# A share of the attention masks moved from TensorE to GpSimd, and the squared norms from GpSimd to ScalarE

## Chip, cores and metric

The kernel runs on one core of a Trainium2 chip. The metric is the device time of one execution in microseconds (us). A core has five engines that run side by side, each through its own queue of instructions in order: TensorE (matrix products, PE in the profile, with its weight loads as PEld), VectorE (DVE), ScalarE (ACT), GpSimd (POOL) and SyncE (SP, which here issues DMA transfers). The engines wait for each other through semaphores.

## What is computed

A block-sparse attention is followed by a layer of experts in which each token goes to one of eight.

```python
# q, k, v: (B=4, H=8, S=768, D=64) float32; 24 blocks of 32 tokens
scores = scale * np.matmul(q, k.transpose(0, 1, 3, 2))
mask = np.abs(blk_i - blk_j) <= 1                      # neighbouring blocks
mask = mask | (blk_i == 0) | (blk_j == 0) | (blk_i == 23) | (blk_j == 23)
#      ... and three sampled key blocks for each query block
attn = softmax(np.where(mask, scores, -1e9)) @ v
x = attn.transpose(0, 2, 1, 3).reshape(3072, 512)
# routing: cosine of each row with 8 expert vectors, softmax, best expert
xn = x / (np.linalg.norm(x, axis=-1, keepdims=True) + 1e-06)
logits = xn @ en.T / tau
expert_idx = np.argmax(logits, axis=1);  gate_w = softmax(logits)[.., expert_idx]
for e in range(8):
    out[rows of e] = gate_w * (np.maximum(x[rows of e] @ w1[e], 0) @ w2[e])
```

The mask is the same for all batches and heads. The scores are small, so the kernel takes the exponential without subtracting a maximum.

## The kernel before

The work of the attention is cut into 192 **units**. One unit is one pair of heads, one half of the queries (384) and one chunk of the keys (128). Six units (kc = 0 to 5) make a **half**: all keys for one pair of heads and one half of the queries. There are 32 halves; eight halves (48 units) make a **sequence**, that is, one of the four batches. A unit has two TensorE parts, `score_fast` and `attend_fast`. Between them stands the exponential on ScalarE.

```python
def score_fast(k, u):
    ps = k.big.tile([P, 2, 512], F32, name="sc", tag="big")        # PSUM, 2 buffers
    quarters = [(h, r, ...) for r in range(2) for h in range(2)]
    for rows, cols, first in ((k.kmask, k.qmask, True), (kt, qt, False)):
        for h, r, keys in quarters:       # mask product in bf16, then scores in f32, summed in PSUM
            nc.tensor.matmul(ps[D*r:D*(r+1), h, 0:HALF], lhsT=rows[D*h:D*(h+1), keys],
                             rhs=cols[D*h:D*(h+1), queries], start=first, stop=not first)
    e = k.ep.tile([P, 2, HALF], F32, name="e", tag="e")            # SBUF, 4 buffers
    k.exps = nc.scalar.activation(e, ps[:, :, 0:HALF], ACT.Exp, scale=SCALE)

def attend_fast(k, u):
    # kc == 0: k.av = new PSUM tile (1 buffer); kc == 1: esum = first + e
    k.summed = nc.vector.tensor_tensor(out=k.esum, in0=k.esum, in1=e, op=ALU.add)
    for r in range(2):
        for h in range(2):
            nc.tensor.matmul(k.av[D*h:D*(h+1), r, 0:HALF], lhsT=v[..., h, kc, :], rhs=e[D*r:D*(r+1), h, :],
                             start=(kc == 0), stop=(kc == NC - 1))
    if kc == NC - 1:
        nc.scalar.copy(out=part, in_=k.av[:, 1, 0:HALF])
        k.summed = nc.vector.tensor_tensor(out=at, in0=k.av[:, 0, 0:HALF], in1=part, op=ALU.add)
```

The mask product adds a large negative number to the scores of forbidden blocks, so that their exponential is zero. `settle` then turns a finished half back to rows with tokens on partitions (36 small matmuls), and divides by the sums of the exponentials. `squares` adds up the squares of the new rows for the norm.

```python
def settle(k, w):
    ...                                                            # 12 + 24 matmuls into PSUM "back"
    nc.vector.reduce_sum(out=den.rearrange(...), in_=sums, axis=AX.X)
    nc.vector.tensor_scalar(out=den, in0=den, scalar1=1e-9, scalar2=None, op0=ALU.add)
    nc.vector.reciprocal(out=inv..., in_=den)
    nc.vector.tensor_tensor(out=k.x[b][...], in0=rows[:, :, :, 0:D], in1=inv..., op=ALU.mult)
    nc.vector.tensor_tensor(out=k.part[b][...], in0=rows[:, :, :, D:W], in1=inv..., op=ALU.mult)

def squares(k, w):                                                 # the last half uses ScalarE instead
    nc.gpsimd.tensor_tensor(out=sq, in0=x, in1=x, op=ALU.mult)     # 128 x 384
    width = P // 2
    while width:                                                   # 7 steps of a tree, 192 down to 3
        nc.gpsimd.tensor_tensor(out=out, in0=sq[:, :, 0:width], in1=sq[:, :, width:2*width], op=ALU.add)
        width //= 2
```

The main loop keeps the scores two units ahead. In the first unit of a half the score stands ahead of the other part, because the one buffer of `av` must first be read out by `at`.

```python
for u in range(units):
    if u % NC == 3 and ...: settle(n, u // NC - 1)
    if u % NC == 4 and ...: squares(n, u // NC - 1)
    for when, what in plan: ...                                    # routing and dispatch of the sequence before
    steps = [partial(attend_fast, n, u)] + ([partial(score_fast, n, u + 2)] if u + 2 < units else [])
    for step in reversed(steps) if u % NC == 0 else steps:
        step()
    if u % per - ... in (0, 1): turn_blocks(...)                   # DVE transposes of the next pair
```

After the attention come 25 **tiles** of 128 rows each: gather the rows of one expert, two products with its weights (`hp`, `yp`), scatter the result. Four more tiles stand behind a condition and run only if the routing needs them; `last_tiles` then fetches their rows itself.

```python
def fetch(k, i):
    if i + 2 < k.stop and i + 2 != NE:
        fetch_rows(k, i + 2)             # late tiles: four indirect DMAs on GpSimd
```

Of the kernel before, what the change touches and what calls it, by code (L numbers as in the profile page):

```python
# [45 lines left out]
XE = P + 1  # L46
XW = ND * XE
SCALE = 1.0 / float(D) ** 0.5
HALF = S // 2
NQ = HALF // P  # L50
DEN_LOW, DEN_HIGH = 0.1, 1e10
NEG = -1.0e9


class Net:
# [3 lines left out]
def two_banks(k, name):  # L59
    return k.small.tile([P, 2, 512], F32, name=name, tag="small")  # L60
# [300 lines left out]
def score_fast(k, u):  # L361

    nc = k.nc
    g, qh, kc = u // (2 * NC), u // NC % 2, u % NC
    kt, qt = k.turned[g]
    ps = k.big.tile([P, 2, 512], F32, name="sc", tag="big")
    queries = slice(qh * HALF, (qh + 1) * HALF)
    quarters = [(h, r, slice(kc * P + D * r, kc * P + D * (r + 1))) for r in range(2) for h in range(2)]
    for rows, cols, first in ((k.kmask, k.qmask, True), (kt, qt, False)):
        for h, r, keys in quarters:  # L370
            nc.tensor.matmul(ps[D * r:D * (r + 1), h, 0:HALF], lhsT=rows[D * h:D * (h + 1), keys],  # L371
                             rhs=cols[D * h:D * (h + 1), queries], start=first, stop=not first)
    e = k.ep.tile([P, 2, HALF], F32, name="e", tag="e")
    k.exps = nc.scalar.activation(e, ps[:, :, 0:HALF], ACT.Exp, scale=SCALE)  # L374
    k.es[u] = e


def attend_fast(k, u):
# [24 lines left out]
def settle(k, w):  # L403

    nc = k.nc
    at, esum = k.done.pop(w)
    g, qh = w // 2, w % 2
    b, j = g // NPAIR, g % NPAIR
    if w % (2 * NPAIR) == 0:
        k.x[b] = k.xp.tile([P, NC, ND, XE], F32, name="x", tag="x")  # L410
        k.nsq[b] = k.xp.tile([P, NC, NPAIR], F32, name="nsq", tag="nsq")
        k.part[b] = k.xp.tile([P, NC, H, E], F32, name="part", tag="part")
    ps = two_banks(k, "back")
    W = D + E
    rows = ps[:, :, 0:NQ * W].rearrange("p h (t w) -> p t h w", t=NQ)
    sums = ps[:, :, NQ * W:NQ * W + 2 * NQ].rearrange("p r (t h) -> p t h r", t=NQ)
    for t in range(NQ):
        for h in range(2):
            for s in range(2):
                cols = slice(t * P + D * s, t * P + D * (s + 1))  # L420
                nc.tensor.matmul(rows[D * s:D * (s + 1), t, h, :], lhsT=at[D * h:D * (h + 1), cols],  # L421
                                 rhs=k.back[D * h:D * (h + 1), j, :], start=True, stop=True)
    for t in range(NQ):
        for h in range(2):
            for r in range(2):
                for s in range(2):
                    cols = slice(t * P + D * s, t * P + D * (s + 1))
                    nc.tensor.matmul(sums[D * s:D * (s + 1), t, h, r:r + 1], lhsT=esum[D * r:D * (r + 1), h, cols],  # L428
                                     rhs=k.ones[D * r:D * (r + 1), 0:1], start=True, stop=True)
    den = k.dens[:, w, :]  # L430
# [10 lines left out]
    nc.vector.tensor_tensor(out=k.part[b][:, chunks, 2 * j:2 * j + 2, :], in0=rows[:, :, :, D:W],  # L441
                            in1=inv.unsqueeze(3).broadcast_to([P, NQ, 2, E]), op=ALU.mult)


def squares(k, w):

    nc = k.nc
    b, j, qh = w // (2 * NPAIR), w // 2 % NPAIR, w % 2
    chunks = slice(qh * NQ, (qh + 1) * NQ)
    x = k.x[b][:, chunks, j, 0:P]  # L450
    sq = k.sp.tile([P, NQ, P], F32, name="sq", tag="sq", bufs=1)
    nc.gpsimd.tensor_tensor(out=sq, in0=x, in1=x, op=ALU.mult)  # L452
    width = P // 2
    while width:
        out = sq[:, :, 0:width] if width > 1 else k.nsq[b][:, chunks, j:j + 1]
        k.squared = nc.gpsimd.tensor_tensor(out=out, in0=sq[:, :, 0:width], in1=sq[:, :, width:2 * width],  # L456
                                            op=ALU.add).ins
        width //= 2


def last_squares(k, w):

    b, j, qh = w // (2 * NPAIR), w // 2 % NPAIR, w % 2
    for c in range(qh * NQ, (qh + 1) * NQ):
        sq = k.sp.tile([P, P], F32, name="sq_l", tag="sq_l")
# [508 lines left out]
def after_sequence(n, b):  # L974

    routing = partial(next, route(n, b), None)
    plan = [(7, routing), (14, routing), (16, routing), (17, routing), (20, partial(rank, n, b)), (23, routing)]
# [12 lines left out]


def attention_fast(n, ctx):
    def pool(name, bufs, **kw):
        return ctx.enter_context(n.tc.tile_pool(name=name, bufs=bufs, **kw))

    n.acc, n.big = pool("acc", 1, space=PSUM), pool("big_f", 2, space=PSUM)
    n.ld, n.tp, n.ep = pool("ld", 3), pool("tp", 2), pool("ep", 4)
    pairs = B * NPAIR
    units, per = pairs * 2 * NC, 2 * NC
    n.masked, n.zeros = [], None  # L1000
# [22 lines left out]
    load_experts(n)  # L1023
    load_blocks(n, 1)
    load_pair(n, 1, (2,))
    plan, experts = [], build_experts(n)
    for u in range(units):
        g = u // per
        if u % per == 0 and g + 2 < pairs:
            load_pair(n, g + 2, (2,))  # L1030
        if u % NC == 3 and NC < u < units - 2 * NC:
            settle(n, u // NC - 1)
        if u % NC == 4 and NC < u < units - 2 * NC:
            squares(n, u // NC - 1)
        if u in (2, 4, 7):
            with n.tc.issue_after(n.summed.ins), n.tc.issue_after(n.exps.ins):
                next(experts)
# [3 lines left out]
            plan = after_sequence(n, u // (per * NPAIR) - 1)  # L1041
        for when, what in plan:
            if when == u % (per * NPAIR):
                with n.tc.issue_after(n.summed.ins), n.tc.issue_after(n.exps.ins), n.tc.issue_after(n.tick.ins):
                    what()

        steps = [partial(attend_fast, n, u)] + ([partial(score_fast, n, u + 2)] if u + 2 < units else [])
        for step in reversed(steps) if u % NC == 0 else steps:
            step()
        turn = u % per - (0 if g else NC - 1)  # L1050
        if turn in (0, 1) and g + 1 < pairs:
            with n.tc.issue_after(n.summed.ins):
# [5 lines left out]
        if u >= units - 4 and u % 2 == 0:  # L1058
            squares(n, 2 * B * NPAIR - 3 + (u == units - 2))


def attention_exact(n, ctx):
# [70 lines left out]
def fast(n):  # L1133
    n.rings, n.loads, n.squared = {}, 0, None
    with ExitStack() as ctx:
# [74 lines left out]
def kernel(  # L1210
# [14 lines left out]
    n = Net()  # L1225
# [2 lines left out]
    n.emb, n.tau, n.w1, n.w2 = moe_expert_emb, moe_tau, moe_w1, moe_w2  # L1228
    n.loaded, n.vs, n.es, n.ets, n.sums, n.x, n.rows, n.weights = {}, {}, {}, {}, {}, {}, {}, {}

    n.raw, n.turned, n.done, n.part, n.nsq, n.turned_rows = {}, {}, {}, {}, {}, {}
    n.exact = False
    n.const = ctx.enter_context(tc.tile_pool(name="const", bufs=1))
# [41 lines left out]
```

## Time and profile before

| what | value |
|---|---|
| time, median of 3 runs | 700.07 us (700.06 to 700.4) |
| span of the profiled run | 698.1 us, granted TensorE clock 0.99 |
| PE / DVE / ACT / POOL busy | 679.2 / 343.4 / 188.5 / 289.7 us |
| attention, mask products `sc<-qmask,kmask` | 768 instructions, 323 ns each |
| attention, scores `sc<-qt,kt` | 1536 instructions, 482 ns each |
| exponential `e<-sc`, 128x768 | 192 instructions, 811 ns each |
| sums `esum<-esum,e`, 128x768 | 128 instructions, 1002 ns each |
| `squares` on POOL, 8 instructions for a half | 31 halves, first one 993 ns |
| `sq_l` on ACT, 128x128, with an accumulator read | 3 of 300 ns, 3 of 187 ns |

Busy times of matmuls may not be added up: four matmuls of 64 rows and 64 columns run side by side, and their spans overlap. What a matmul costs is read from the start of one group to the start of the next. For the other engines the mean of a row is the time of one instruction, and idle time of an engine costs nothing as long as no other engine waits for it. The busy span of a GpSimd instruction is rough, and holds time in which it cannot proceed.

### The profile page before, as it was taken

What the parts mean: (1) busy time and instruction counts of PE and PEld (TensorE: products, weight loads), DVE (VectorE), ACT (ScalarE), POOL (GpSimd) and SP (SyncE); (2) the same over time, 40 slices, a digit from 0 to 9 for tenths busy, and PEclk for the clock granted to TensorE, in tenths of its full rate; (3) what the DMA queues carried; (4) which work ended last, traced back from release to release, by engine and by line L of the source; (5) the groups of instructions that cost most, each with busy time, mean ns of one, the idle gap of its engine ahead of it and who ended that gap; (6) DMA issues with size and microseconds to landing.
All of it is one profiled execution on the core that took longest, in us unless ns stands there. A gap on an engine that the chain in (4) does not pass through costs nothing.

```text
span 698.1 us, 19311 instructions
## 1 busy us (share of the span) xinstructions
PE 679.2 (97%) x8221; PEld 427.0 (61%) x8221; DVE 343.4 (49%) x734; ACT 188.5 (27%) x266; POOL 289.7 (42%) x442
## 2 busy tenths in 40 slices
PE   9999999999999999999999999999999999999990
PEld 4555555555555555557667776674667746677660
DVE  7887778787888888865752112111221122111200
ACT  5455545554555545552000000000000000000000
POOL 1255466544774468626302442244323432234000
PEclk9999999999999999999999999999999999999995
DMA  7833345674426569644999899999899998999300
GB/s 119 138 66 53 49 65 70 131 179 83 69 50 160 119 158 201 234 152 154 350 402 378 306 335 344 349 320 337 317 399 402 401 376 322 399 407 397 110 18 14
DMA packets 170023, 155.91 MB, mean 223 GB/s; under 512 B 129148, under 2 KB 129148, under 8 KB 167110
## 3 DMA queue, kind: packets, MB, share of 16 engines
q1 hardware_dynamic: 163366, 141.47, 65.4%
q0 software_dynamic: 4960, 12.90, 5.0%
q8 instruction: 66, 1.08, 0.7%
q10 hardware_dynamic: 1600, 0.20, 0.2%
q14 instruction: 31, 0.25, 0.1%
HBM read 138.74 MB, written 16.07 MB: 222 GB/s over the span
## 4 chain that ended last, share of the span: by engine, by line
PE 96%; DMA 1%; DVE 0%; issue 0%; ACT 0%; POOL 0%; POOLq 0%
PE hp L907 24%; PE yp L922 23%; PE sc L371 22%; PE av L393 18%; PE back L428 3%; PE hp L950 2%; PE yp L970 2%; PE back L421 2%; DMA kld<-in_k_dram 0%; PE hp L962 0%; DMA qld<-in_q_dram 0%; PE xg_ps L883 0%; PE slot_ps L669 0%; ACT e L374 0%; PE quarter_ps L686 0%
## 5 line engine op out<-in xcount | busy, mean ns | idle before, releaser
L374 ACT ACTIVATE e<-sc 128x768 f32<-128x768 f32 x192 | 155.7, 811 | 147.0 <-PE sc L371 143.3
L907 PEld LDWEIGHTS hp<-xgt,w 128*128 128x128 f32 x1472 | 167.8, 192 | 10.8 <-issue 10.2
L907 PE MATMUL hp<-xgt,w 128*128 128x128 f32 x1472 | 169.3, 275 | 0.0
L922 PE MATMUL yp<-w,h 128*128 128x512 f32 x368 | 161.7, 592 | 0.0
L371 PE MATMUL sc<-qt,kt 64*64 64x384 f32 x1536 | 158.0, 482 | 0.1
L393 PE MATMUL av<-e,vld 64*64 64x384 f32 x1536 | 154.1, 486 | 0.0
L390 DVE TENSOR_TENSOR esum<-esum,e 128x768 f32<-128x768 f32 x128 | 128.2, 1002 | 32.3 <-ACT e L374 29.1
L922 PEld LDWEIGHTS yp<-w,h 128*128 128x128 f32 x368 | 68.2, 190 | 77.0 <-issue 75.8
L456 POOL TENSOR_TENSOR sq<-sq 128x192 f32<-128x192 f32 (+1 forms) x186 | 103.5, 557 | 13.9
L910 ACT ACTIVATE h<-hp 128x512 f32<-128x512 f32 x23 | 13.7, 597 | 290.8 <-PE hp L907 264.0
L828 POOL DMA_INDIRECT xg<-x_dram,quarter x80 | 80.5, 1006 | 28.1 <-issue 23.2
L931 POOL DMA_INDIRECT out_dram<-y,slot_l x20 | 20.1, 1007 | 169.1 <-DVE y L930 169.1
L914 DVE TENSOR_SCALAR h<-hp 128x512 f32<-128x512 f32 x23 | 15.9, 692 | 147.8 <-PE hp L907 147.8
L393 PEld LDWEIGHTS av<-e,vld 64*64 64x64 f32 x1536 | 55.1, 133 | 53.6 <-issue 26.5
L371 PEld LDWEIGHTS sc<-qt,kt 64*64 64x64 f32 x1536 | 58.8, 133 | 38.9 <-issue 36.0
L452 POOL TENSOR_TENSOR sq<-x 128x384 f32<-128x384 f32 x31 | 30.8, 993 | 112.4 <-DVE part L441 96.5
L371 PE MATMUL sc<-qmask,kmask 64*64 64x384 bf16 x768 | 65.9, 323 | 0.1
L930 DVE TENSOR_SCALAR y<-yp,gate 128x512 f32<-128x512 f32 x20 | 15.0, 751 | 83.5 <-PE yp L922 71.4
L371 PEld LDWEIGHTS <-kmask 64*64 64x64 bf16 x768 | 24.7, 107 | 33.0 <-issue 33.0
L388 DVE TENSOR_TENSOR esum<-e 128x768 f32<-128x768 f32 x32 | 31.4, 981 | 7.1 <-ACT e L374 7.1
L428 PE MATMUL back<-ones,esum 64*64 64x1 f32 x1536 | 26.4, 190 | 0.0
L428 PEld LDWEIGHTS back<-ones,esum 64*64 64x64 f32 x1536 | 25.6, 135 | 0.0
(206 smaller groups left out, 354.8 us busy)
## 6 DMA issues: line engine op xcount, KB each, us to landing
w<-in_moe_w_dram SPq DMA_DIRECT2D x50, 2048.0 KB
w<-in_moe_w_dram SPq DMA_DIRECT2D x16, 512.0 KB
x_dram<-x SPq DMA_DIRECT2D x24, 258.0 KB
vld<-in_v_dram SPq DMA_DIRECT2D x32, 192.0 KB
kld<-in_k_dram SPq DMA_DIRECT2D x60, 96.0 KB
qld<-in_q_dram SPq DMA_DIRECT2D x60, 96.0 KB
x_early<-x SPq DMA_DIRECT2D x12, 258.0 KB
xg<-x_dram,quarter POOLq DMA_INDIRECT x80
```

The costliest lines, as they stand in the source:

```text
L371: nc.tensor.matmul(ps[D * r:D * (r + 1), h, 0:HALF], lhsT=rows[D * h:D * (h + 1), keys], rhs=cols[D * h:D * (h + 1), queries], start=first ...
L374: k.exps = nc.scalar.activation(e, ps[:, :, 0:HALF], ACT.Exp, scale=SCALE)
L388: k.summed = nc.vector.tensor_tensor(out=k.esum, in0=k.first, in1=e, op=ALU.add)
L390: k.summed = nc.vector.tensor_tensor(out=k.esum, in0=k.esum, in1=e, op=ALU.add)
L393: nc.tensor.matmul(k.av[D * h:D * (h + 1), r, 0:HALF], lhsT=v[D * r:D * (r + 1), h, kc, :], rhs=e[D * r:D * (r + 1), h, :], start=(kc == 0 ...
L428: nc.tensor.matmul(sums[D * s:D * (s + 1), t, h, r:r + 1], lhsT=esum[D * r:D * (r + 1), h, cols], rhs=k.ones[D * r:D * (r + 1), 0:1], star ...
L452: nc.gpsimd.tensor_tensor(out=sq, in0=x, in1=x, op=ALU.mult)
L456: k.squared = nc.gpsimd.tensor_tensor(out=out, in0=sq[:, :, 0:width], in1=sq[:, :, width:2 * width], op=ALU.add).ins
L828: k.nc.gpsimd.indirect_dma_start(out=x[:, g], out_offset=None, in_=quarters, in_offset=bass.IndirectOffsetOnAxis(ap=k.quarter[:, g, t:t + ...
L907: nc.tensor.matmul(hp[:, f, :], lhsT=w1[:, d, (f0 + f) * P:(f0 + f + 1) * P], rhs=xt[:, d, :], start=(d == 0), stop=(d == ND - 1))
L922: nc.tensor.matmul(yp, lhsT=h[:, f, :], rhs=w2[:, f, :], start=(f == 0), stop=(f == NF - 1))
L931: k.scattered = nc.gpsimd.indirect_dma_start(out=k.out[:, :], out_offset=bass.IndirectOffsetOnAxis(ap=slot, axis=0), in_=y[:, :], in_offse ...
```

## The change

The change has five parts.

1. **Masks by multiplication.** In the units kc = 1 and kc = 4 of some halves, the four mask products are left out, and GpSimd multiplies the exponential in place with a tile of ones and zeros (`cut`, bf16), which is built once with two groups of four matmuls and two activations. `WHOLE` lists the units of a sequence that keep the mask product; they lie where GpSimd has routing or dispatch. This leaves 32 units out of 192: 12 in the first sequence, 11 in the second, 3 in the third and 6 in the fourth. Of these, 17 have kc = 1 and 15 have kc = 4.
2. **Scores three units ahead** instead of two, with five buffers of `e` instead of four, so that the multiplication has room.
3. **Squares on ScalarE**: three activations with an accumulator for each half, where GpSimd had eight instructions.
4. **`settle` is split**: its VectorE part becomes `divide` and comes at kc = 5, behind `at`; the sum of two columns is now two instructions of another kind.
5. **Rows of two conditional tiles are gathered ahead** in the last two unconditional tiles: eight more indirect DMAs on GpSimd. The conditional part still fetches its own rows.

```diff
+AHEAD = 3
+CUT = (1, 4)
+WHOLE = {1: range(10, 24), 2: range(10, 2 * NC * NPAIR), 3: (*range(24), 43, 46)}
 def score_fast(k, u):
-    for rows, cols, first in ((k.kmask, k.qmask, True), (kt, qt, False)):
+    cut = g > 0 and kc in CUT and u % (2 * NC * NPAIR) not in WHOLE.get(g // NPAIR, ())
+    for rows, cols, first in ((k.kmask, k.qmask, True), (kt, qt, False))[int(cut):]:
     ...
+    if cut:
+        mask = k.cut[:, CUT.index(kc), queries].unsqueeze(1).broadcast_to([P, 2, HALF])
+        k.squared = nc.gpsimd.tensor_tensor(out=e, in0=e, in1=mask, op=ALU.mult).ins
+def build_cut(k, i):
+    ...   # 4 matmuls kmask x qmask, then activation(Relu, bias=1.0, scale=-10.0 / NEG)
+def divide(k, w):   # the VectorE part of settle
-    nc.vector.reduce_sum(out=den.rearrange("p (t h) -> p t h", t=NQ), in_=sums, axis=AX.X)
-    nc.vector.tensor_scalar(out=den, in0=den, scalar1=1e-9, scalar2=None, op0=ALU.add)
+    nc.vector.tensor_scalar(out=per_row, in0=sums[:, :, :, 0], scalar1=1e-9, scalar2=None, op0=ALU.add)
+    nc.vector.tensor_tensor(out=per_row, in0=sums[:, :, :, 1], in1=per_row, op=ALU.add)
 def squares(k, w):
-    nc.gpsimd.tensor_tensor(out=sq, in0=x, in1=x, op=ALU.mult)
-    ...   # the tree
+    for c in range(qh * NQ, (qh + 1) * NQ):
+        k.nc.scalar.activation(sq, k.x[b][:, c, j, 0:P], ACT.Square, accum_out=k.nsq[b][:, c, j:j + 1])
 def fetch(k, i):
-    if i + 2 < k.stop and i + 2 != NE:
+    if i + 2 != NE:
 # main loop
-        if u % NC == 4 and NC < u < units - 2 * NC:
-            squares(n, u // NC - 1)
+        if u in (3, 5):
+            build_cut(n, u // 2 - 1)
-        steps = [partial(attend_fast, n, u)] + ([partial(score_fast, n, u + 2)] if u + 2 < units else [])
+        scored = u + (AHEAD if u > NC else 2)
+        steps = [partial(attend_fast, n, u)] + [partial(score_fast, n, i) for i in range(ahead, ...)]
+        if u % NC == 5 and NC < u < units - 2 * NC:
+            divide(n, u // NC - 1)
+        if u % NC == 1 and 2 * NC < u < units - NC:
+            squares(n, u // NC - 2)
 # behind the attention, in the first tile
-            last_squares(n, 2 * B * NPAIR - 1)
+            divide(n, 2 * B * NPAIR - 1)
+            for w in (3, 2, 1):
+                squares(n, 2 * B * NPAIR - w)
```

More of the change, by code (lines that the diff above doesn't have):

```diff
@@ L368, in score_fast @@
     quarters = [(h, r, slice(kc * P + D * r, kc * P + D * (r + 1))) for r in range(2) for h in range(2)]
-    for rows, cols, first in ((k.kmask, k.qmask, True), (kt, qt, False)):
+    cut = g > 0 and kc in CUT and u % (2 * NC * NPAIR) not in WHOLE.get(g // NPAIR, ())
+    for rows, cols, first in ((k.kmask, k.qmask, True), (kt, qt, False))[int(cut):]:
         for h, r, keys in quarters:
             nc.tensor.matmul(ps[D * r:D * (r + 1), h, 0:HALF], lhsT=rows[D * h:D * (h + 1), keys],
-                             rhs=cols[D * h:D * (h + 1), queries], start=first, stop=not first)
+                             rhs=cols[D * h:D * (h + 1), queries], start=first or cut, stop=not first)
     e = k.ep.tile([P, 2, HALF], F32, name="e", tag="e")
     k.exps = nc.scalar.activation(e, ps[:, :, 0:HALF], ACT.Exp, scale=SCALE)
+    if cut:
+        mask = k.cut[:, CUT.index(kc), queries].unsqueeze(1).broadcast_to([P, 2, HALF])
+        k.squared = nc.gpsimd.tensor_tensor(out=e, in0=e, in1=mask, op=ALU.mult).ins
     k.es[u] = e
+def build_cut(k, i):
+    nc = k.nc
+    if i == 0:
+        k.cut = k.const.tile([P, len(CUT), S], BF16, name="cut")
+    ps = two_banks(k, "cut_ps")
+    for h in range(2):
+        for r in range(2):
+            rows = slice(D * h, D * (h + 1))
+            nc.tensor.matmul(ps[D * r:D * (r + 1), h, 0:HALF],
+                             lhsT=k.kmask[rows, CUT[i] * P + D * r:CUT[i] * P + D * (r + 1)],
+                             rhs=k.qmask[rows, h * HALF:(h + 1) * HALF], start=True, stop=True)
+    nc.scalar.activation(k.cut[:, i].rearrange("p (h t) -> p h t", h=2), ps[:, :, 0:HALF], ACT.Relu, bias=1.0,
+                         scale=-10.0 / NEG)
 def attend_fast(k, u):
@@ L408, in settle @@
     b, j = g // NPAIR, g % NPAIR
[L409 to L412, printed above, removed]
     ps = two_banks(k, "back")
@@ L429, in settle @@
                                      rhs=k.ones[D * r:D * (r + 1), 0:1], start=True, stop=True)
+    k.settled[w] = rows, sums
+def divide(k, w):
+    nc = k.nc
+    rows, sums = k.settled.pop(w)
+    g, qh = w // 2, w % 2
+    b, j = g // NPAIR, g % NPAIR
+    W = D + E
+    if w % (2 * NPAIR) == 0:
+        k.x[b] = k.xp.tile([P, NC, ND, XE], F32, name="x", tag="x")
+        k.nsq[b] = k.xp.tile([P, NC, NPAIR], F32, name="nsq", tag="nsq")
+        k.part[b] = k.xp.tile([P, NC, H, E], F32, name="part", tag="part")
     den = k.dens[:, w, :]
-    nc.vector.reduce_sum(out=den.rearrange("p (t h) -> p t h", t=NQ), in_=sums, axis=AX.X)
-    nc.vector.tensor_scalar(out=den, in0=den, scalar1=1e-9, scalar2=None, op0=ALU.add)
+    per_row = den.rearrange("p (t h) -> p t h", t=NQ)
+    nc.vector.tensor_scalar(out=per_row, in0=sums[:, :, :, 0], scalar1=1e-9, scalar2=None, op0=ALU.add)
+    nc.vector.tensor_tensor(out=per_row, in0=sums[:, :, :, 1], in1=per_row, op=ALU.add)
     k.tick = nc.sync.dma_start(out=k.ticks[w:w + 1, :], in_=den[0:1, 0:1])
@@ L445, in squares @@
 def squares(k, w):
[L447 to L461, printed above, removed]
     b, j, qh = w // (2 * NPAIR), w // 2 % NPAIR, w % 2
     for c in range(qh * NQ, (qh + 1) * NQ):
-        sq = k.sp.tile([P, P], F32, name="sq_l", tag="sq_l")
+        sq = k.sp.tile([P, P], F32, name="sq", tag="sq")
         k.nc.scalar.activation(sq, k.x[b][:, c, j, 0:P], ACT.Square,
@@ L976, in after_sequence @@
     routing = partial(next, route(n, b), None)
-    plan = [(7, routing), (14, routing), (16, routing), (17, routing), (20, partial(rank, n, b)), (23, routing)]
+    plan = [(8, routing), (14, routing), (16, routing), (17, routing), (20, partial(rank, n, b)), (23, routing)]
     plan += [(27 + NC * (i // 4), routing) for i in range(NC * (1 + (b < EARLY)))]
@@ L996, in attention_fast @@
     n.acc, n.big = pool("acc", 1, space=PSUM), pool("big_f", 2, space=PSUM)
-    n.ld, n.tp, n.ep = pool("ld", 3), pool("tp", 2), pool("ep", 4)
+    n.ld, n.tp, n.ep = pool("ld", 3), pool("tp", 2), pool("ep", 5)
     pairs = B * NPAIR
@@ L1025, in attention_fast @@
     load_pair(n, 1, (2,))
-    plan, experts = [], build_experts(n)
+    plan, experts, ahead = [], build_experts(n), 2
     for u in range(units):
@@ L1043, in attention_fast @@
             if when == u % (per * NPAIR):
-                with n.tc.issue_after(n.summed.ins), n.tc.issue_after(n.exps.ins), n.tc.issue_after(n.tick.ins):
+                with n.tc.issue_after(n.summed.ins), n.tc.issue_after(n.exps.ins), n.tc.issue_after(n.tick.ins), \
+                        n.tc.issue_after(n.squared):
                     what()
-        steps = [partial(attend_fast, n, u)] + ([partial(score_fast, n, u + 2)] if u + 2 < units else [])
+        scored = u + (AHEAD if u > NC else 2)
+        steps = [partial(attend_fast, n, u)] + [partial(score_fast, n, i) for i in range(ahead, min(scored + 1, units))]
+        ahead = scored + 1
         for step in reversed(steps) if u % NC == 0 else steps:
             step()
+        if u % NC == 5 and NC < u < units - 2 * NC:
+            with n.tc.issue_after(n.summed.ins):
+                divide(n, u // NC - 1)
+        if u % NC == 1 and 2 * NC < u < units - NC:
+            with n.tc.issue_after(n.exps.ins):
+                squares(n, u // NC - 2)
         turn = u % per - (0 if g else NC - 1)
@@ L1057, in attention_fast @@
             settle(n, u // NC - 1)
-        if u >= units - 4 and u % 2 == 0:
-            squares(n, 2 * B * NPAIR - 3 + (u == units - 2))
+            divide(n, u // NC - 1)
 def attention_exact(n, ctx):
@@ L1229 @@
     n.loaded, n.vs, n.es, n.ets, n.sums, n.x, n.rows, n.weights = {}, {}, {}, {}, {}, {}, {}, {}
+    n.settled = {}
     n.raw, n.turned, n.done, n.part, n.nsq, n.turned_rows = {}, {}, {}, {}, {}, {}
```

## The prediction, made before the changed kernel ran

> **What bounds the kernel now.** I read the chain of waits first, then the slices, then busy times by stage, then the timeline of one half. From the page, the chain and two rows of the slices (40 equal parts of the span):
>
> ```profile
> PE 96%; DMA 1%; DVE 0%; issue 0%; ACT 0%; POOL 0%; POOLq 0%
> ...
> PE   9999999999999999999999999999999999999990
> ...
> PEclk9999999999999999999999999999999999999995
> ```
>
> TensorE is the bound from the second slice to the last but one, at full clock. The table of windows splits that into attention, tiles and end (window; its length; then busy time of PE, PEld, DVE, ACT, POOL with counts; clock, DMA share, GB/s):
>
> ```profile
> 16.00:322.00 306.00, 306.00 (x5974) 170.94 (x5966) 245.79 (x482) 162.63 (x220) 169.23 (x290) 1.00 0.54 114
> 322.00:681.30 359.30, 358.72 (x2112) 249.39 (x2108) 85.69 (x216) 17.81 (x35) 116.13 (x131) 1.00 0.90 331
> 681.30:698.10 16.80, 0.00 (x0) 0.00 (x0) 0.67 (x1) 0.00 (x0) 0.97 (x1) 0.57 0.04 14
> ```
>
> So the attention up to 322 us has no TensorE gap, and only TensorE time that is left out, or a new gap, can move the end. Whether "busy" is also full rate is seen in the timeline, TensorE alone (start, length, line):
>
> ```profile
> 92.34 0.34 PE L371 MATMUL sc<-qmask,kmask 64*64 64x384 bf16 x4
> 92.50 0.82 PE L371 MATMUL sc<-qt,kt 64*64 64x384 f32 x8
> 93.14 0.82 PE L393 MATMUL av<-e,vld 64*64 64x384 f32 x8
> 93.79 0.34 PE L371 MATMUL sc<-qmask,kmask 64*64 64x384 bf16 x4
> 93.95 0.82 PE L371 MATMUL sc<-qt,kt 64*64 64x384 f32 x8
> 94.60 0.82 PE L393 MATMUL av<-e,vld 64*64 64x384 f32 x8
> ```
>
> The lengths overlap; the distances of the starts are the cost. Mask 92.34 to 92.50 = 0.16 us, scores 0.64, `av` 0.65, in all 1.45 for a unit. `settle` costs 1.04 (90.62 to 91.66 in the same timeline). A half is then 6 x 1.45 + 1.04 = 9.74, and 32 halves make 312, which is the attention. It runs at its own matmul rate.
>
> **What the Trainium skill says.** "TensorEngine Tiling (Array Packing)", Key Properties: tiles of the array work independently, so matmuls in different ones run in parallel. The trace agrees: four mask products of 323 ns each, one group every 0.16 us. This is why a mask is worth 0.16 us and not 1.3.
>
> "GPSIMD Engine Reference", section 3.1: two-input elementwise work takes about 2.6 cycles an element, measured 4497 ns for 2048, that is 2.2 ns each. The trace: shortest spans 0.38 us for 96 elements and 0.59 for 192, slope 2.2, but 0.82 for 384, slope 1.2. From 0.82 upwards with these two slopes, 768 elements take 1.28 to 1.67 us; 2.2 x 768 is 1.69. No run here has a bf16 second operand of that size. I take **1.65 us, an estimate**.
>
> The same page, section 8 (Key points): GpSimd shares its SBUF interfaces with VectorE and collides with VectorE instructions that have two SBUF inputs. The trace agrees:
>
> ```profile
> 64.55 0.83 POOL L452 TENSOR_TENSOR sq<-x 128x384 f32<-128x384 f32 x1 [4.20 <-DVE part L441]
> 64.93 1.26 DVE L390 TENSOR_TENSOR esum<-esum,e 128x768 f32<-128x768 f32 x1 [0.41 <-ACT e L374]
> ```
>
> `esum` takes 0.96 alone and 1.26 here, as if it began its work 0.30 late, near the end of the GpSimd span. These two exclude each other, nearly whole instruction by whole instruction.
>
> **The change, part by part.**
>
> 1. Mask products: 32 units x 0.161 = **5.15 us** less on TensorE. `build_cut` adds 2 x 0.16 = **0.32**. Net 4.8 us, if nothing waits.
>
> 2. The wait that can come in: `av` of a cut unit now needs score, exponential and GpSimd product. For kc = 1, TensorE does between the end of its score and its `av`: `av` (0.645), score (0.805), score (0.805), `av` (0.645) = 2.90 us, with the score three units ahead and in the order of the built instruction list. The exponential starts 0.25 after the matmuls have been issued (94.84 against 94.60), takes 0.81, and the next engine starts 0.04 later: 1.10. From a release to the `av` matmul are 0.19 (weight load at 96.67, matmul at 96.86), plus 0.04. This leaves 2.90 - 1.10 - 0.23 = **1.57 us for the product**. With 1.65 it is late by 0.08. In some halves GpSimd first waits for an `esum` of 0.96; I lay out one half with both instructions exclusive and find about **0.14 us** of stall for a kc = 1 unit: 17 x 0.14 = 2.4 us.
> For kc = 4 a `settle` lies in between: 2.90 + 1.06 = 3.96, which leaves 2.63 us. I take no stall there.
>
> 3. VectorE: 7.63 us busy in a half (mean of the two from 81.6 to 101.2, routing included), of which 4.8 `esum`. A cut half adds 2 x 1.65 = 3.3 of GpSimd that excludes `esum`: 8.1 in 9.42. The rest of VectorE (`at`, `divide`, transposes) reads PSUM or one SBUF input, and can lie beside the product. It fits, without much room. The GpSimd tree that collided before (31 x 8 instructions, 143 us in the rows of lines 452 and 456) is gone.
>
> 4. Squares on ScalarE: 3 x (0.300 + 0.187) = 1.46 us for a half. ScalarE is 5.25 busy in 9.8, so 6.7 in 9.42. They stand behind the exponential of kc = 4 and delay that of kc = 5 by some 0.9; before its `av` lie a `settle`, two `av` and two scores, so this is covered. The tables need no reload: one table load in the whole trace, though it has both exponentials and squares.
>
> 5. `divide`: two small instructions of 0.16 each for two others, off the path. Behind the attention, two more halves of squares run on ScalarE during the first tile; they can start before the last `divide`, so the routing chain, which ends close to its matmul (`seen` ends 337.86, `rk` starts 337.94), should not grow. Eight more gathers of 1.0 us lie on GpSimd inside tiles of 14.0 us, which hold five such instructions already; the last scatter, at 682.25, comes long after. Zero.
>
> Sum: -5.15 + 0.32 + 2.4 = -2.4 us. That would be 697.6. The list of excluded units is fine-grained (two single units of the last half), as if those that did not pay had been removed. I go a little lower: **697.0 us**.
>
> **The rivals.**
>
> - *All of the product is hidden.* For it: the 1.2 slope gives 1.28 us, well under 1.57. Then -4.8: 695.2 us.
> - *The product becomes the wait.* If a bf16 operand costs more, or the collision hits each product, 2.0 us means 0.4 late in the wait of step 2, and laid out with the exclusion 0.6 a half and more, since the delayed `esum` then holds up `at` and with it the next `av`. 16 halves x 0.67 = 10.7 of loss against 4.8: 706. Against it: in the kernel before, GpSimd spent 3.7 to 4.4 us a half on colliding work with no TensorE gap. For it: nothing waited for that work.
> - *VectorE becomes the bound* in cut halves: 7.6 + 3.3 = 10.9 if nothing lay side by side, 1.5 over 9.42. Half of that is 12 us. Not likely, since PSUM readers lie beside it.
> - *The tiles eat it.* If the attention ends earlier, weights could come late. Against it: no TensorE wait for a DMA in the list of waits, and tiles take 14.0 us with 4 MB each, 10.6 us at the 395 GB/s of 360 to 380 us.
>
> **Range and chances.** The step that carries the uncertainty is the length of the product: from 695.2 (hidden) over 697.6 (1.65) to 706 (2.0, worst case). I set 694.8 to 701.0 for 8 in 10. Two per cent is 14 us, three times all the mask time removed: 1% faster, 97% within, 2% slower.
>
> **What the changed profile would show.** Step 1: mask products down from 768 to 640, and TensorE in cut halves 9.42 us apart. Step 2: weight loads of `av` waiting for the product on GpSimd, some 17 waits of 0.1 to 0.3 us, none for kc = 4; product about 1.65 us. Step 3: `esum` longer by up to the product's length where they meet, but no longer wait for `at`. Step 4: ScalarE up by some 45 us, no second table load. Step 5: tiles of 14.0 us and an end of 16.8 as before. I would be wrong if the product takes over 1.9 us, if `av` at kc = 0 waits for `at` much longer than the 9.3 us in total of now, or if the start of the routing behind the attention opens a TensorE gap.

## The result, and the profile after

The changed kernel takes **688.44 us** (median of six runs, 688.22 to 689.04) against 700.17 for the kernel before: ratio 0.9833, 95% interval 0.9821 to 0.9846. The prediction was 697.0, range 694.8 to 701.0. The gain is 11.7 us, nearly four times the predicted one.

The page first: the TensorE row and the clock of the slices, and the chain by engine.

```profile
PE   9999999999999999999999999999999999999995
...
PEclk9999999999999999999999999999999999999999
...
PE 97%; POOL 1%; ACT 1%; issue 0%; DVE 0%; POOLq 0%; ACTq 0%
```

TensorE still is the bound, and GpSimd has come into the chain with 1%. What differs most is easy to miss: in the last slice the TensorE row shows 5 instead of 0, and the clock 9 instead of 5. The table of windows, cut at the first tile's matmul and just behind the last one (same columns as before):

```profile
16.00:320.45 304.45, 303.98 (x5858) 172.50 (x5847) 249.34 (x482) 186.09 (x401) 93.37 (x84) 1.00 0.50 116
320.45:679.70 359.25, 358.70 (x2112) 249.38 (x2108) 85.57 (x216) 18.70 (x41) 118.94 (x129) 1.00 0.90 331
679.70:686.60 6.90, 0.00 (x0) 0.00 (x0) 0.71 (x1) 0.00 (x0) 1.01 (x1) 0.88 0.09 33
```

The tiles are the same to a tenth (359.17 us from the first `hp` to the end of the last `yp`, in both traces). The attention ends 1.56 us earlier. The stretch behind the last matmul, where no engine computes anything but the last `y` and its scatter, fell **from 16.93 to 6.97 us, by 9.96**. So of the 11.5 us between the two profiles, about 10 lie in the part that the prediction took as fixed.

What is in that stretch is seen when the instructions of a single line are listed, the engines' queues included (columns: duration of one in ns as min/median/max, then first and last start). POOLq is GpSimd's sequencer. Of the kernel before:

```profile
L1241 POOLq INC_SWDGE_SEM  x1: 2388/2388/2388, 685.8 to 685.8; - x1
L1270 POOLq DRAIN  x3: 40/107/9061, 688.2 to 697.8; - x3
```

and of the changed kernel:

```profile
L1274 POOLq INC_SWDGE_SEM  x1: 428/428/428, 684.2 to 684.2; - x1
L1303 POOLq DRAIN  x3: 40/107/1057, 684.7 to 686.3; - x3
```

Neither is an operation that the kernel asks for: the first carries the line of the condition behind which the four late tiles stand, the second the line of the `with` that encloses the whole program. A semaphore step took 2.39 us and now takes 0.43; the longest of three drains took 9.06 and now takes 1.06. Together 11.45 and 1.49: a difference of 9.96, the whole of it.

The parts aimed at show in the timeline of a half with two cut units, TensorE alone (the fast case of the prediction):

```profile
44.73 0.82 PE L378 MATMUL sc<-qt,kt 64*64 64x384 f32 x8
45.38 0.82 PE L419 MATMUL av<-e,vld 64*64 64x384 f32 x8
46.02 0.82 PE L378 MATMUL sc<-qt,kt 64*64 64x384 f32 x8
46.67 0.82 PE L419 MATMUL av<-e,vld 64*64 64x384 f32 x8
47.31 0.34 PE L378 MATMUL sc<-qmask,kmask 64*64 64x384 bf16 x4
```

The score at 46.02 starts 0.64 us behind `av`, with no mask group between, and the next steps follow at the old distances: the mask is gone and nothing took its place here. The groups of the page (busy us, mean ns of one, idle time before and its releaser), with the product at 1.79 us in the mean:

```profile
L416 DVE TENSOR_TENSOR esum<-esum,e 128x768 f32<-128x768 f32 x128 | 142.3, 1112 | 9.7 <-ACT e L381 2.3
...
L384 POOL TENSOR_TENSOR e<-e,cut 128x768 f32<-128x768 f32 x32 | 57.2, 1788 | 114.1 <-ACT e L381 114.1
...
L488 ACT ACTIVATE sq<-x 128x128 f32<-128x128 f32 x96 | 28.3, 299 | 7.2 <-DVE x L476 7.2
```

### The profile page after: what moved, and what is told of

Read it like the earlier page. It is cut to its first block, busy times and chain, and to the rows that moved or that the text cites. A ratio compares the mean times of both kernels' runs of the same rounds, so it can differ in the third digit from the quotient of the medians.

```text
span 686.6 us, 19070 instructions
## 1 busy us (share of the span) xinstructions
PE 677.3 (99%) x8101; PEld 428.5 (62%) x8101; DVE 346.8 (51%) x734; ACT 213.6 (31%) x454; POOL 216.7 (32%) x234
## 3 DMA queue, kind: packets, MB, share of 16 engines
q8 instruction: 65, 1.06, 0.6%
## 4 chain that ended last, share of the span: by engine, by line
PE 97%; POOL 1%; ACT 1%; issue 0%; DVE 0%; POOLq 0%; ACTq 0%
PE hp L929 24%; PE yp L944 23%; PE sc L378 21%; PE av L419 18%; PE back L450 3%; PE yp L992 2%; PE hp L972 2%; PE back L443 2%; PE warm L88 1%; POOL e L384 1%; ACT e L381 0%; PE hp L984 0%; PE xg_ps L905 0%; PE slot_ps L691 0%; PE quarter_ps L708 0%
## 5 line engine op out<-in xcount | busy, mean ns | idle before, releaser
L419 PE MATMUL av<-e,vld 64*64 64x384 f32 x1536 | 156.7, 487 | 0.4 <-DVE at L425 0.2
L416 DVE TENSOR_TENSOR esum<-esum,e 128x768 f32<-128x768 f32 x128 | 142.3, 1112 | 9.7 <-ACT e L381 2.3
L850 POOL DMA_INDIRECT xg<-x_dram,quarter x88 | 88.4, 1004 | 32.3 <-issue 27.1
L384 POOL TENSOR_TENSOR e<-e,cut 128x768 f32<-128x768 f32 x32 | 57.2, 1788 | 114.1 <-ACT e L381 114.1
L378 PEld LDWEIGHTS sc<-qt,kt 64*64 64x64 f32 x1536 | 61.3, 133 | 40.4 <-issue 38.0
L378 PE MATMUL sc<-qmask,kmask 64*64 64x384 bf16 x640 | 56.6, 323 | 0.1
L378 PEld LDWEIGHTS <-kmask 64*64 64x64 bf16 x640 | 22.2, 107 | 26.0 <-issue 18.6
L425 DVE TENSOR_TENSOR at<-av,part 128x384 f32<-128x384 f32 x32 | 17.8, 557 | 36.7 <-ACT part L423 36.4
L556 POOL TENSOR_TENSOR part<-part 128x192 f32<-128x192 f32 (+1 forms) x8 | 7.6, 955 | 78.9 <-DVE part L479 78.6
L488 ACT ACTIVATE sq<-x 128x128 f32<-128x128 f32 x96 | 28.3, 299 | 7.2 <-DVE x L476 7.2
```

Of the source, the lines that this page charges most:

```text
L384: k.squared = nc.gpsimd.tensor_tensor(out=e, in0=e, in1=mask, op=ALU.mult).ins
L419: nc.tensor.matmul(k.av[D * h:D * (h + 1), r, 0:HALF], lhsT=v[D * r:D * (r + 1), h, kc, :], rhs=e[D * r:D * (r + 1), h, :], start=(kc == 0 ...
L850: k.nc.gpsimd.indirect_dma_start(out=x[:, g], out_offset=None, in_=quarters, in_offset=bass.IndirectOffsetOnAxis(ap=k.quarter[:, g, t:t + ...
```

## The experiments

**What was to be told apart.** The theory: the eight extra gathers of part 5 shorten the end. Its first rival: parts 1 to 4 do it, since they take 31 x 8 computing instructions from GpSimd, whose drain it is. Within the theory there are two more: what counts is the number of indirect DMAs on GpSimd, or it is that some are issued late, close to the end. The second question is what parts 1 to 4 do to the attention.

### Part 5 undone, and part 5 alone

```diff
 # e1: the changed kernel
-    if i + 2 != NE:
+    if i + 2 < k.stop and i + 2 != NE:
 # e2: the kernel before
-    if i + 2 < k.stop and i + 2 != NE:
+    if i + 2 != NE:
```

> The changed kernel without its fifth part: the two conditional tiles are not gathered ahead, all else stays. The changed profile has its last matmul only 1.56 us earlier than before, but the stretch behind it is 6.97 us instead of 16.93; there the last reset instruction and the drain on GpSimd take 0.43 + 1.06 us instead of 2.39 + 9.06. Theory A (the extra gathers shorten that stretch): about 698.5 us, stretch near 17 us. Theory B (moving the squares off GpSimd, or another part, shortens it): about 688.4 us, stretch near 7 us.

> The kernel before with the fifth part alone: one condition taken out, eight more gathers. Theory A: about 690 us, all of it from the stretch behind the last matmul (near 7 us), attention as before (first tile at 322.0 us). Theory B: 700 us, stretch near 17 us.

Measured: without part 5, 698.25 us, ratio 0.9970 [0.9958, 0.9981]; part 5 alone, 690.35 us, ratio 0.9858 [0.9842, 0.9875]. The same line of both, e1 and then e2:

```profile
L1303 POOLq DRAIN  x3: 40/107/9061, 686.8 to 696.4; - x3
```

```profile
L1270 POOLq DRAIN  x3: 40/107/1057, 686.5 to 688.1; - x3
```

The long drain comes and goes with part 5, to the nanosecond, and GpSimd's computing has no part in it: e1 has the changed kernel's GpSimd, e2 that of before. The two effects add up: 2.16 us (e1 against its kernel before, 700.41) and 10.06 (e2) make 12.2; the whole change gave 11.7.

### Half of part 5

```diff
 # e4: the kernel before, with the rows of one conditional tile instead of two
-    if i + 2 < k.stop and i + 2 != NE:
+    if i + 2 <= k.stop and i + 2 != NE:
```

> The kernel before with only the first of the two tiles gathered ahead: four more gathers on GpSimd in the last tile but one, none in the last, so that GpSimd is idle for 13 us ahead of its last scatter as in the kernel before. If a recent gather on GpSimd is what shortens the end: 700 us, as before. If any more gathers or another count do it: about 690 us.

Measured: 691.68 us, ratio 0.9876 [0.9860, 0.9893]. The semaphore step took 0.348 us and the drain 0.731, less than with eight; yet the stretch behind the last matmul is 8.21 us, longer than the 6.95 of e2. So the end isn't shortened in proportion to the gathers: four are enough to cross some edge, and behind it more of them cost again. And something new waits. The timeline of GpSimd near the end, first the changed kernel (the number in brackets is the idle time before):

```profile
666.68 1.01 POOL L953 DMA_INDIRECT out_dram<-y,slot_l  x1 [7.75 <-DVE y L952]
669.76 1.03 POOL L850 DMA_INDIRECT xg<-x_dram,quarter  x1 [2.08 <-issue]
671.09 1.00 POOL L850 DMA_INDIRECT xg<-x_dram,quarter  x1 [0.30 <-issue]
```

and that of e4:

```profile
668.69 1.01 POOL L931 DMA_INDIRECT out_dram<-y,slot_l  x1 [7.76 <-DVE y L930]
684.18 1.00 POOL L931 DMA_INDIRECT out_dram<-y,slot_l  x1 [14.48 <-issue]
```

Counted from the start of the program, the instruction with 2.08 us before it is the 114th indirect DMA of the changed kernel. In e4 the 114th is the last scatter, whose row had been ready: it starts 2.5 us behind the end of the last `yp`, in e2 1.1. That is most of the 1.7 us by which e4's end is longer than its short step and drain would make it (6.95 - 0.08 - 0.33 = 6.5).

### The number, or the lateness

```diff
 # f1, f3, f4: the kernel before; tile 12 gathers rows again, long before the end
-            for g in range(NG):
+            for g in (*range(NG), *range(NG), *range(NG)) if i == 12 else range(NG):   # f1: 118 DMAs
+            for g in (*range(NG), 0) if i == 12 else range(NG):                        # f3: 111
+            for g in (*range(NG), 0, 1) if i == 12 else range(NG):                     # f4: 112
 # f2: e2 (eight late gathers), with those of tiles 12 and 13 left out: 110 again
+            for g in () if i in (12, 13) else range(NG):
```

f2 computes two tiles with old rows, but it does the same matmuls. f1 to f4 ran once each, and so did g1 and g2 below; the step and the drain repeat to the nanosecond wherever the number is the same, the times don't.

> The kernel before with eight more gathers, but in the middle: the four gathers of tile 12 are done three times over, into the same buffer with the same rows. The kernel before ends with 110 indirect DMAs on GpSimd and 11.45 us in its last reset and drain; with 118 (changed kernel) it was 1.49, with 114 (half of the fifth part) 1.08. Theory A1 (the number of indirect DMAs decides): 118 here too, reset and drain near 1.5 us, about 690 us. Theory A2 (a gather late in the kernel decides; here three scatters follow the last gather, as in the kernel before): near 11.5 us, 700 us.

> The kernel before with the fifth part, but the eight gathers of tiles 12 and 13 left out, so that these tiles compute with the rows that an earlier tile left in their buffers and the output is not the reference's. The number is 110 as in the kernel before, the last two tiles have gathers as in the changed kernel. Theory A1 (number): reset and drain near 11.5 us, 700 us. Theory A2 (late gather): near 1.5 us, 690 us.

> The kernel before with one gather of tile 12 done twice: 111 indirect DMAs, the end as before. Theory A1 (number): if 110 is a special number, near 1.5 us in reset and drain and 690 us; if there is a threshold between 111 and 114, near 11.5. Theory A2 (late gather): 11.5 us, 700 us.

> The kernel before with two gathers of tile 12 done twice: 112 indirect DMAs, the end as before. Theory A1: as with 111, or the side of a threshold on which 112 lies. Theory A2: 11.5 us, 700 us.

| run | indirect DMAs | semaphore step, us | drain, us | stretch behind the last matmul, us | time, us |
|---|---|---|---|---|---|
| before | 110 | 2.388 | 9.061 | 16.93 | 700.17 |
| f2: eight late, eight left out | 110 | 2.388 | 9.061 | 17.06 | 700.94 |
| f3 | 111 | 2.408 | 9.142 | 17.19 | 700.95 |
| f4 | 112 | 2.428 | 9.224 | 17.19 | 700.77 |
| e4 | 114 | 0.348 | 0.731 | 8.21 | 691.68 |
| f1: eight in the middle | 118 | 0.428 | 1.057 | 7.17 | 693.57 |
| e2 | 118 | 0.428 | 1.057 | 6.95 | 690.35 |
| changed kernel | 118 | 0.428 | 1.057 | 6.97 | 688.44 |

It is the number, or something that is counted along with each gather. f1 has no late gather and a short drain; f2 has all the late gathers and the long one. f1's time is 3 us above e2's because its re-gathers hold up the tiles (362.2 us instead of 359.2), not because of its end. Below the edge each DMA adds 0.020 us to the step and 0.082 to the drain; between 112 and 114 both collapse.

### Far below the edge, and far above

```diff
 # g1: the kernel before; five tiles don't gather and compute with old rows
+            for g in () if i in (12, 13, 14, 15, 16) else range(NG):
 # g2: the changed kernel, two tiles gathered twice
+            for g in (*range(NG), *range(NG)) if i in (12, 14) else range(NG):
```

> The kernel before with the gathers of five tiles left out: 90 indirect DMAs instead of 110 (the output is not the reference's in those tiles). Theory: below the 114th DMA the reset and the drain at GpSimd's end grow with each DMA issued, by 0.020 and 0.083 us. Then the reset is 0.15 + 90 x 0.0204 = 1.99 us, the drain 90 x 0.083 = 7.5 us, the stretch behind the last matmul about 16.95 - 2.0 = 15.0 us, the time about 698. Rival, only the crossing of a number counts and the end is flat below it: 2.39 and 9.06, 17.0 us, 700.

> The changed kernel with eight more gathers in the middle of the tiles (two tiles gathered twice): 126 indirect DMAs. Theory: counting starts anew at the 114th and goes on with the same slope, so reset 0.43 + 8 x 0.0204 = 0.59 us, drain 1.06 + 8 x 0.083 = 1.72 us, the stretch behind the last matmul 6.97 + 0.8 = 7.8 us; the tiles may be longer by up to 3 us from the gathers. Rival, beyond the crossing the end is short and flat: 0.43 and 1.06, 7.0 us.

Measured: g1, 698.29 us, step 1.988, drain 7.427, stretch 15.06; g2, 689.09 us, step 0.588, drain 1.711, stretch 7.99.

```profile
L1270 POOLq DRAIN  x3: 40/107/7427, 688.3 to 696.3; - x3
```

```profile
L1303 POOLq DRAIN  x3: 40/107/1711, 684.8 to 687.1; - x3
```

Twenty DMAs fewer save 1.634 us of drain, 0.0817 each; eight more than 118 cost 0.654, again 0.0817 each. One law fits all fourteen programs of this case within 4 ns: drain = 0.074 + 0.0817 n us, step = 0.188 + 0.0200 n us. Up to 112, n is the number of indirect DMAs; from 114 on it is that number less 106. It is as if at the 114th the count of 106 earlier ones had been cleared.

The 114th has a price of its own, and its size depends on what stands around it. In all eight programs that reach the 114th it waits, with nothing in the profile that it waits for. In g2 it stands inside a group of gathers:

```profile
641.06 1.00 POOL L850 DMA_INDIRECT xg<-x_dram,quarter  x1 [0.30 <-issue]
642.54 1.00 POOL L850 DMA_INDIRECT xg<-x_dram,quarter  x1 [0.48 <-issue]
643.85 1.00 POOL L850 DMA_INDIRECT xg<-x_dram,quarter  x1 [0.30 <-issue]
```

It costs 0.18 us there (0.49 for 0.31 in f1), against 1.8 as the first gather behind a scatter and 1.5 as the last scatter. Only the last of these is on the path.

### The mask product left out

```diff
 # e3: the changed kernel without part 1
-    cut = g > 0 and kc in CUT and ...
+    cut = False and kc in CUT and ...
-        if u in (3, 5):
-            build_cut(n, u // 2 - 1)
 # ... and the order behind the last product, which no longer exists, is dropped
```

> The changed kernel with all masks as matmuls again and the mask tile not built; score three ahead, squares on ScalarE, split settle and gathers stay. The prediction's sum puts the cut at -4.83 + 2.4 = -2.4 us, so this kernel should start its first tile 2.4 us later than the changed one (322.9 us against 320.45), and take about 690.8 us with the short end. Rival 1 (all products hidden): 4.8 later, 693.2. Rival 2 (the cut brings nothing, squares and the rest do): no later, 688.4.

Measured: 691.10 us, ratio 0.9869 [0.9852, 0.9885]. From the first `av` matmul to the first of the tiles it takes 313.84 us, before 312.70, in the changed kernel 310.91. So parts 2 to 4 are not free: they **cost 1.1 us**, and part 1 brings 2.9. Where the cost lies is seen in the distances from one `settle` to the next: the three halves with the `rank` step of routing grew from 10.11 or 10.13 to between 10.29 and 10.32, and one that has a dispatch step in the same place from 10.34 to 10.51, 0.76 in all. `settle` writes to a PSUM buffer that `rank` used just before, and VectorE reads `rank`'s result late. The read in the timeline of VectorE, before and then e3:

```profile
118.92 0.17 DVE L584 COPY count<-rk 128x8 f32<-128x8 f32 x1
```

```profile
118.94 2.04 DVE L416 TENSOR_TENSOR esum<-esum,e 128x768 f32<-128x768 f32 x2
120.90 0.16 DVE L606 COPY count<-rk 128x8 f32<-128x8 f32 x1
```

The `rk` products start at 118.65 and 119.48. Before, the read began 0.27 us later; in e3 two sums stand ahead of it, and it begins 1.42 later. VectorE works in order, and `divide` in its new place behind `at` (1.2 us) has pushed the sums back into that gap; the next runs test this.

A part of what part 1 costs is seen here too. From the first `av` to the first `settle` e3 takes 13.60 us and the changed kernel 14.38, though no unit is cut so early. The mask tile is built there, and its two activations stand on ScalarE ahead of `part`. The changed kernel, then e3:

```profile
17.19 0.81 ACT L400 ACTIVATE cut<-cut_ps 128x768 bf16<-128x768 f32 x1
...
18.40 0.56 DVE L425 TENSOR_TENSOR at<-av,part 128x384 f32<-128x384 f32 x1 [1.34 <-ACT part L423]
...
19.01 0.88 PE L419 MATMUL av<-e,vld 64*64 64x384 f32 x8 [0.23 <-DVE at L425]
```

```profile
17.31 0.56 DVE L425 TENSOR_TENSOR at<-av,part 128x384 f32<-128x384 f32 x1 [0.47 <-ACT part L423]
...
17.39 0.84 PE L378 MATMUL sc<-qt,kt 64*64 64x384 f32 x8
...
18.04 0.84 PE L419 MATMUL av<-e,vld 64*64 64x384 f32 x8
```

In e3 `av` follows its scores after 0.65 us. In the changed kernel these scores start at 17.94, so that `av` could begin at 18.59; it begins at 19.01, behind `at`. With its two groups of matmuls (0.32) `build_cut` so costs **0.78 us**.

### `divide` back behind `settle`

```diff
 # g3: the changed kernel; g4: the same, and one gather instead of four for the second conditional tile
         if u % NC == 3 and NC < u < units - 2 * NC:
             settle(n, u // NC - 1)
+            divide(n, u // NC - 1)
-        if u % NC == 5 and NC < u < units - 2 * NC:
-            with n.tc.issue_after(n.summed.ins):
-                divide(n, u // NC - 1)
 # g4 alone
-            for g in range(NG):
+            for g in range(NG if i <= k.stop else 1):
```

> The changed kernel with divide directly behind settle again (its place as in the kernel before, its new two instructions kept). Theory: divide behind at pushes the sums and with them the readout of the rank product on VectorE, which holds up the settle of five halves by 0.2 us more. Then those halves fall from 10.3 to 10.1, the attention from 313.5 to about 312.5, the time from 688.4 to about 687.5. Rival, the longer halves come from the scores three units ahead or from the squares on ScalarE: nothing changes, 688.4. Second rival: with divide early the masked units of GpSimd meet more VectorE work and stalls grow, 689 or more.

> The same with only five gathers ahead of the conditional tiles instead of eight: 115 indirect DMAs. Theory: the wait of 2.1 us on the 114th DMA falls on a gather that nobody waits for, and the drain is shorter by 3 x 0.083, the reset by 3 x 0.020: the stretch behind the last matmul about 6.7 us instead of 6.97, the time 0.3 us below that of the same kernel with eight. Rival: the wait falls too close to the last scatter and comes out at the end, 8 us or more for that stretch.

Measured: g3, 687.16 us (686.97 to 687.59), ratio 0.9812 [0.9796, 0.9829]; g4, 687.20, ratio 0.9811 [0.9794, 0.9827]. The halves with `rank` are back at 10.11, the one with dispatch at 10.34: together 0.75 us less than in the changed kernel. What the expectation didn't have: four cut halves of 9.70 to 9.77 are now 9.55 or 9.56, another 0.7. One went the other way, from 13.98 to 14.23: its second product took 2.01 us instead of 1.76. Why the four are shorter is seen in the timeline of one kc = 1 unit, in the changed kernel and then in g3:

```profile
57.33 1.90 POOL L384 TENSOR_TENSOR e<-e,cut 128x768 f32<-128x768 f32 x1 [3.61 <-ACT e L381]
...
58.39 1.77 PE L419 MATMUL av<-e,vld 64*64 64x384 f32 x16
```

```profile
57.45 1.65 POOL L384 TENSOR_TENSOR e<-e,cut 128x768 f32<-128x768 f32 x1 [3.56 <-ACT e L381]
...
58.54 1.52 PE L419 MATMUL av<-e,vld 64*64 64x384 f32 x16
```

With `divide` late, the last `esum` of the half still runs when the product begins, the product takes 0.25 us longer, and the two groups of `av` behind it stretch by the same 0.25. With `divide` early, VectorE reads PSUM beside the product. From the first `settle` to the tiles g3 takes 294.99 and g4 295.02 us, the changed kernel 296.53 (296.21 in e1, 296.19 in g2). That is 1.2 to 1.5 us, in line with 1.28 between the medians. The ratios of g3 and of the changed kernel overlap; the halves settle it, which are alike in the two traces with `divide` early and alike in the three with it late. These two have the lowest times found here.

g4's end was as expected: step 0.368, drain 0.812, 6.71 us behind the last matmul (7.07 in g3). In the times this 0.3 us doesn't show; it is smaller than the spread of the runs.

## Why the prediction was wrong, point by point

**The step that failed is step 5**, in its last word: eight more gathers "lie on GpSimd inside tiles of 14.0 us ... Zero", and "an end of 16.8 as before". The gathers do lie hidden there, as it said. But the end was taken as a constant because no engine was busy in it. Of its 16.9 us, 11.45 were two instructions of GpSimd's sequencer, plain in the trace of before once the line is listed with its queues, and they depend on how many indirect DMAs went before. This term was set to 0 and measured -10. Nothing in the trace of before alone showed the edge at 114, so its sign couldn't have been read there; that the end held an unexplained 11 us on the very engine whose DMAs were changed could.

**The rest was sized to within a microsecond, partly by luck.** The sum for the attention was -2.4, so 697.6; the changed kernel without part 5 took 698.25. In the traces part 1 brought 2.9 instead of 2.4, parts 2 to 4 cost 1.1 instead of nothing, and inside part 1 two more terms were off in opposite directions:

- *Step 1*: 640 mask products are left, as it said, and most halves with two cut units are 9.46 to 9.52 us long (9.46 would follow from the measured half of 9.79; the text's 9.42 came from its slightly short 9.74). But building the mask tile cost 0.78 us, not 0.32: the sum had its matmuls and not its two activations of 0.8 us on ScalarE.
- *Step 2*: stalls of 2.4 us were predicted. Against halves of 9.46, the stalls in the cut halves add up to about 1.6. They aren't even, 0.14 for each kc = 1 unit: mostly it is 0.06 and less for a half, 0.23 to 0.31 in four of them (1.1 together), where a sum still ran for 0.4 us when the product of kc = 1 began, and 0.16 in one near the end. The estimate of the product, 1.65 us, was right for a product that isn't held up: 18 of the 32 took 1.64 to 1.66. Eleven took 1.76 to 1.90 and three 2.44, so that the mean is 1.79.
- *Step 3*: `esum` grew from 1002 to 1112 ns, as it said. "No longer wait for `at`" holds for TensorE, not for VectorE. In the waits (us in total, times, longest) the changed kernel has

```profile
DVE at L425 <- ACT part L423: 36.4, 26, 3.4
...
PEld av L419 <- POOL e L384: 9.9, 21, 0.7
...
PEld av L419 <- DVE at L425: 9.6, 29, 0.9
```

  VectorE's wait ahead of `at` grew from 15.1 to 36.4 us, but little of it reaches TensorE, whose wait for `at` is 9.6 against 9.3. The middle line is the new wait of step 2: all 17 units with kc = 1, and four of those with kc = 4, for which none was expected. It is the weight loader's idle time, six times the 1.6 us that the halves lost.
- *Step 4*: no second table load, no stall, as it said. "ScalarE up by some 45 us" was too much: 25.1 (188.5 to 213.6). The rows of the squares do sum to 45 more, but an activation overlaps with its accumulator read, and the read with the next activation: three take 0.97 us, not 1.46, and overlap the work around them besides.
- *Step 5, first half*: `divide` "off the path" was wrong too. Its new place holds up `settle` in the four halves with `rank` or dispatch, 0.75 us in all, through the order of VectorE, and lengthens the product in four others; g3 took both back. The 0.75 is most of the 1.1 us that parts 2 to 4 cost in e3. Of the rest, 0.19 lies in one half of 9.98 us. The start is 0.82 longer, where one more mask and score (0.80) now stand ahead of the first `settle`, and the end 0.65 shorter. Neither was tested, nor was the first routing step of a sequence, which the changed kernel also has one unit later.

**The rivals.** None named the end. "The tiles eat it" failed as argued: the tiles are 359.17 in both. "The product becomes the wait" is what four of the halves show in small.

**The sources of the estimates, against the traces.** The figure of the Trainium skill, "GPSIMD Engine Reference", section 3.1, carried the product: 2.2 ns an element makes an estimate of 1.69 us, and the median here is 1.656. Its section 8, on GpSimd contending with VectorE instructions that have two SBUF inputs, fits what g3 shows: 1.90 us where a sum still ran at the start, 1.65 where none did. On the end, the skill's "VectorE: DVE Perf Modes", The DRAIN you can't avoid, speaks of drains of about 12 ns, constant, on all five engines, that stand before and behind a kernel. At the end of the kernel before, those of SyncE, ScalarE and the weight loader took 7 to 13 ns, VectorE's 10 and 135, and GpSimd's 40, 107 and 9061; whether the page means these drains isn't known, but for the last one the measurement decides. The skill's "DMA: Bandwidth & Descriptors", SWDGE vs HWDGE vs iDMA, says that for DMAs issued from GpSimd its cores compute the descriptors and append them to rings. A ring that is tidied up, either during the program or at its end, would fit the numbers above. No run here looked into it, so this is a guess.

**What stays open**: what is cleared at the 114th, why 106 of them, whether 113 is still long, and whether the edge lies in the number of DMAs or in something that goes with it, such as their descriptors. Only gathers were added and left out, never scatters.

## What to carry to other kernels

Open the stretch behind the last computing instruction as you would any other, with the sequencers' instructions listed: here 11.5 of 700 us stood there, a cost of each indirect DMA that no row of busy times shows. If it grows with a number, try that number on both sides, fewer and more; here twenty DMAs fewer took 1.9 us off the end, and eight useless ones more took off 10, because 110 happened to lie just below an edge. On an engine that works in order, an operation that is moved off the path still pushes what stands behind it; look at who reads a buffer last, and when.

## What the runs showed of the hardware that was not expected

- The end of this program grows with the indirect DMAs that GpSimd has issued, by 0.102 us each (0.0817 drain, 0.0200 semaphore step) up to 112: 9.4 us in both at 90, 11.45 at 110.
- Between 112 and 114 it falls to 1.1 us, and then grows at the same rate: 1.49 at 118, 2.30 at 126. The 114th DMA waits once, from 0.18 us inside a group of gathers to 1.8 behind a scatter.
- A product of 128x768 f32 with a bf16 mask takes GpSimd 1.656 us in the median, 2.16 ns an element, and up to 2.44 where sums of VectorE run beside it. No run has two f32 operands of this size, so what the bf16 operand does to the time isn't shown.
- A square with an accumulator on ScalarE, 128x128, takes 0.30 us and its read 0.19, but the two together span 0.39, and one square follows the other every 0.29.
